# Agent attention with a top-1 mixture of experts: the second layer's high and low products into the same columns

## The chip, the cores and the metric

One NeuronCore of a Trainium2 chip runs the whole kernel. The metric is device microseconds for one execution, as the median of several runs. PE (TensorE) multiplies matrices into PSUM, which has eight banks of 512 float32 per partition; ACT (ScalarE), DVE (VectorE) and POOL (GpSimd) work on 128 partitions beside it, POOL on SBUF alone here; SP (SyncE) issues most DMAs. A matmul on PE has its stationary operand ("weights") loaded first by a separate instruction, which the profile lists as an engine of its own, PEld.

## The reference

Four batches of 11,456 tokens with 128 channels go through attention to 49 agents, and the result through a mixture of eight experts of which each token uses one.

```python
a2k = softmax(scale * agents @ k.T)          # 49 agents over the keys
agent_v = a2k @ v
x = softmax(scale * q @ agents.T) @ agent_v  # 45824 tokens x 128
logits = x @ w_gate
e = argmax(logits)                           # one expert for a token
gate_w = softmax(logits)[e]
eom = sigmoid(x @ w_output_gate)[e]
h = relu(x @ w1[e])                          # 1024 hidden
out = gate_w * eom * (h @ w2[e])             # 128
```

All of it is float32.

## The kernel before, in words

For each batch the kernel finds the expert that most tokens of the batch use (the dominant one) and runs every token through it. Tokens of other experts are gathered, run through their own expert in float32 and scattered over the result later: the left-over path (`left_...`, tiles `let`, `lx`, `lh`, `ly`, `lw`, `bigs`). Its index tables are made from gathers with indirect DMAs on POOL and comparisons on DVE.

A batch has twelve units of up to 1,024 tokens. For each unit there are small float32 products with 50 columns: `ks` (agents by keys), `av` (weights by values), `qs` (queries by agents). DVE, ACT and POOL make softmax weights of them; a DMA turns those (`x_ld<-e`), and a half-precision product with 36 columns, `lg`, gives gates and logits. From these comes `smt`, one factor for each token, which holds the softmax's denominator, the gates and the scaling of the half-precision operands.

The main work is two layers on 92 tiles of up to 512 tokens (four groups of 128, a few of 96 or fewer groups), all in half precision with each float32 operand as a high and a low part.

- First layer, `mm1`: half a tile's hidden units at a time, four blocks of 128, in the four PSUM banks 0 to 3: four matmuls `h<-x_ld,w` with 128 rows, then four with 19 rows. Then `relu` makes of each block `hh` (ACT, the high part) and `hl` (DVE, the low part: relu less hh). A ring of 16 blocks (`RING`), two tiles, holds them.
- Second layer, `mm2(i, k, f)`: hidden block f of tile i, in two passes k over the eight blocks, each for 256 tokens (two groups j). A pass has a PSUM bank `y`; group j has 256 columns of it. For each j one matmul takes hh as weights and 256 columns of `vv` (w2's high part, then its low part), and one takes hl as weights and the 128 columns of the high part, into the first 128 columns. These two matmuls are called a step below; there are 2,880 steps.
- `finish(i, k)`: ACT copies the low columns (`ys`), DVE adds them to the high columns (`os`), and the bank is free. After the second pass `store` waits for `smt`, POOL multiplies the tile by it, and SP stores it.

The order on every engine is set when the program is built, by a planner (`Clock`, `Engine`). It keeps a virtual time for each engine, with a cost for each instruction, and issues an instruction when its inputs are ready by that time. Main stream: `main_stream` issues a second-layer block while the first layer is more than `OFF` = 8 blocks ahead, otherwise half a tile of the first layer if there is room in the ring and the four banks are free by the plan. After each matmul `tick` lets one float32 product through ("heavy") or some light work; it stands between the two matmuls of a step. So small products are spread between second-layer matmuls. All work goes through one helper, so the profile's line is L193 for nearly everything, and groups are told apart by tile names.

Of the kernel before, what the change touches and what calls it, by code (L numbers as in the profile page):

```python
# [7 lines left out]
F32 = mybir.dt.float32  # L8
# [3 lines left out]
AF = mybir.ActivationFunctionType  # L12
ALU = mybir.AluOpType
# [3 lines left out]
P = 128  # L17
B, N, C, A, E, F = 4, 11456, 128, 49, 8, 1024
A2 = 50
NB = F // P  # L20
# [2 lines left out]
NTOK = B * N  # L23
SCALE = 1.0 / float(C) ** 0.5

YS = 2

LARGE, SMALL, KEEP = 8, 8, 4
PHASES = [(0, 3, 13, 384), (3, 1, 1, 128)]
# [5 lines left out]
G4 = 4  # L35
# [207 lines left out]
def agent_attention_top1_moe(ctx, tc, qT, kT, v, aT, wg, wo, w1, w2, cst, out):  # L243
    nc = tc.nc
    clk = Clock()
    ACT, DVE, POOL = Engine(clk, "ACT", nc.scalar), Engine(clk, "DVE", nc.vector), Engine(clk, "POOL", nc.gpsimd)
    PE, SY = Engine(clk, "PE", nc.tensor), Engine(clk, "SP", nc.sync)

    def pool(name, bufs):
        return Tiles(clk, ctx.enter_context(tc.tile_pool(name=name, bufs=bufs)), bufs)  # L250
# [3 lines left out]
    wk = pool("wk", 2)  # L254
# [34 lines left out]
    def release(k):  # L289
        banks[k][0] = True  # L290
# [130 lines left out]
    SM = {}  # L421
# [5 lines left out]
    def spawn(g, prio=2):  # L427
        streams.append([prio, len(streams), g, None])
        streams.sort(key=lambda x: x[0])

    def tick(heavy=1, light=2):

        clk.slots = [heavy, 0]
        for x in list(streams):
            if x[3] is not None and x[3][0] == "PE" and clk.can(x[3], x[0]):
                step(x)
        clk.slots = [0, light]
        for x in list(streams):
# [558 lines left out]
    tiles = []  # L997
# [4 lines left out]
    NT = len(tiles)  # L1002
    OFF = 8
    RING = 16
    H = {}
    Y = {}
    done, summed = set(), set()

    def mm1(i, hf):

        b, u, h, pp, n = tiles[i]
        w = pp * n
        own_, rest = state[b]["w"][hf]
        x1, x2 = (x[:, 512 * h:512 * h + w] for x in X1[b, u])
        p = []
        for g in range(G4):
            p.append((bank(f"h{i}_{hf}_{g}", k=g), hold()))
            PE.matmul(p[g][0][:, 0:w], own_[:, g * P:(g + 1) * P], x1, start=True, stop=False)
            if g < G4 - 1:
# [18 lines left out]
        release(mark)  # L1038
        H[i, f] = hh, hl

    def mm2(i, k, f):

        b, u, h, pp, n = tiles[i]
        hh, hl = H[i, f] if 2 * k + 2 < n else H.pop((i, f))
        vv = state[b]["vv"][f // 4]
        if f == 0:
            Y[i, k] = bank(f"y{i}_{k}"), hold()
        for j in range(2):
            y = Y[i, k][0][0:pp, j * 2 * C:(j + 1) * 2 * C]
            sl = slice((2 * k + j) * pp, (2 * k + j + 1) * pp)  # L1050
            PE.matmul(y, hh[:, sl], vv[:, f % 4].rearrange("p h c -> p (h c)"), start=(f == 0 and j == 0),
                      stop=False)
            tick()
            PE.matmul(y[:, 0:C], hl[:, sl], vv[:, f % 4, 0, :], start=False, stop=(f == NB - 1 and j == 1))
            tick(0, 1)
        if f == NB - 1:
            spawn(finish(i, k), 0)

    OS = {}

    def finish(i, k):
        b, u, h, pp, n = tiles[i]
        if k == 0:
            while i > 3 and i - 4 not in done or i > 1 and i - 2 not in summed:
                yield None
            OS[i] = wk.tile([P, 4, C], F32, name=f"os{i}", tag="os", bufs=4)
        os = OS[i]
        y, mark = Y.pop((i, k))
        yv = y.rearrange("p (j h c) -> p j h c", h=2, c=C)
        ol = wk.tile([P, 2, C], F32, name=f"ys{i}_{k}", tag="ys", bufs=YS)  # L1070
        yield from ACT.q.copy(ol[0:pp], yv[0:pp, :, 1, :])
        yield from DVE.q.tensor_tensor(os[0:pp, 2 * k:2 * k + 2, :], yv[0:pp, :, 0, :], ol[0:pp], op=ALU.add)
        release(mark)
        if 2 * k + 2 == n:
            summed.add(i)
            spawn(store(i, os))

    def store(i, os):
        b, u, h, pp, n = tiles[i]
        while (b, u) not in SM:  # L1080
            yield None
        smt = SM[b, u]
        yield from POOL.q.tensor_tensor(os[0:pp, 0:n, :], os[0:pp, 0:n, :],
                                        smt[0:pp, 4 * h:4 * h + n].unsqueeze(2).broadcast_to([pp, n, C]),
                                        op=ALU.mult)
        base, _, nt = UNITS[u]
        r0 = b * N + base
        dst = out[r0:r0 + pp * nt, :].rearrange("(p t) c -> p t c", t=nt)[:, 4 * h:4 * h + n, :]
        yield from SY.q.dma_start(dst, os[0:pp, 0:n, :])
        done.add(i)  # L1090

    def main_stream():
        first_ = [(i, hf) for i in range(NT) for hf in range(2)]
        second_ = [(i, k, f) for i in range(NT) for k in range(tiles[i][4] // 2) for f in range(NB)]
        m1 = m2 = freed = 0
        while m2 < len(second_):
            can1 = can2 = False
            now = clk.now()
            if m1 < len(first_) and G4 * (m1 + 1) - freed <= RING and group_free() is not None and group_free() <= now + 20.0:
                i, hf = first_[m1]  # L1100
                b, u, h, pp, n = tiles[i]
                can1 = (b, u) in X1 and rests[NU * b + u] > 1 and b in state and len(state[b]["w"]) > hf
                can1 = can1 and clk.at([*X1[b, u], *state[b]["w"][hf]]) <= now + 20.0
            i, k, f = second_[m2]
            if (i, f) in H:
                vv = state[tiles[i][0]]["vv"]
                can2 = len(vv) > f // 4 and clk.at([H[i, f][1], vv[f // 4]]) <= now
                can2 = can2 and (f > 0 or n_free() > 1)
            if can2 and (G4 * m1 > NB * i + (NB * k + f) / (tiles[i][4] // 2) + OFF or not can1):
                mm2(i, k, f)  # L1110
                m2 += 1
                if (i, f) not in H:
                    freed += 1
# [408 lines left out]
```

## Time and profile before

| | |
|---|---|
| median of 3 runs | 1071.93 us (1071.73 to 1074.43) |
| the profiled execution's own time | 1073.62 us |
| its span, first to last instruction | 1071.6 us |
| busy: PE, DVE, ACT, POOL | 1033.2, 859.9, 592.6, 275.2 us |
| mean granted TensorE clock | 0.984 |
| instructions | 27,654 |

A page of the profile describes one execution. A group row gives line, engine, operation, output and inputs with sizes, the count, then busy time and the mean of one in ns, then the idle time ahead of such instructions and who ended it. A row of the waits gives who waited for whom, the total, how often, and the longest. A row of the timeline gives start, duration, engine and operation. Records of matmuls overlap, since they are pipelined: the distance from start to start says what a matmul costs. Some matmul records are missing from a trace.

The granted clock is 1.0 for most of the span. PE has work from the first stage, in which keys are loaded and the first agents are made, to the end, since `AHEAD`, `MIX` and the planner spread the batches' small products over the second layer's steps.

### The profile page before, as it was taken

How to read it: one execution, taken by the hardware profiler on the slowest of the kernel's cores; microseconds unless marked ns; L12 is line 12 of the kernel's file. 1: busy time of each engine (PE TensorE's matmuls, PEld its weight loads, DVE VectorE, ACT ScalarE, POOL GpSimd, SP SyncE). 2: the span in 40 equal slices, each digit the busy share in tenths (PEclk: the TensorE clock that was granted, in tenths of full speed). 3: DMA queues.
4: the chain of work that ended last, by engine and by line, in shares of the span. 5: the costliest groups of instructions: out<-in, count | busy, mean ns of one | idle time of the engine just before them, and what ended most of it. 6: DMA issues, size and time to landing. Idle time of an engine off the chain costs nothing. (4 is left out here: it accounts for less than half of the span.)

```text
span 1071.6 us, 27654 instructions
## 1 busy us (share of the span) xinstructions
PE 1033.2 (96%) x10671; PEld 840.9 (78%) x10671; DVE 859.9 (80%) x2344; ACT 592.6 (55%) x1396; POOL 275.2 (26%) x440
## 2 busy tenths in 40 slices
PE   9989899999999999999999999999899999999996
PEld 9977777788788877778788788777677676788885
DVE  2738699888988898888988888989989978877551
ACT  2325456565755665556755665556645554655552
POOL 0301123222121232232121232321123263521121
PEclk9999899999999999999999999999999998999998
DMA  8785854444557444453466544446232732644430
GB/s 293 231 213 156 193 117 146 125 122 136 133 141 197 141 134 112 119 147 116 111 185 166 153 125 119 129 123 171 73 75 56 168 92 78 149 136 130 131 124 28
DMA packets 108818, 147.13 MB, mean 137 GB/s; under 512 B 61128, under 2 KB 71548, under 8 KB 108682
## 3 DMA queue, kind: packets, MB, share of 16 engines
q1 hardware_dynamic: 107338, 143.83, 48.4%
q0 software_dynamic: 1344, 1.49, 0.8%
q8 instruction: 85, 1.39, 0.5%
q14 instruction: 51, 0.42, 0.1%
HBM read 91.86 MB, written 35.17 MB: 119 GB/s over the span
## 5 line engine op out<-in xcount | busy, mean ns | idle before, releaser
L193 PE MATMUL y<-vv,hh 128*128 128x256 f16 (+1 forms) x2880 | 593.0, 275 | 4.3 <-DVE w L193 3.1
L193 PE MATMUL y<-vv,hl 128*128 128x128 f16 (+1 forms) x2880 | 532.7, 220 | 3.3 <-DVE hl L193 2.5
L193 DVE SCALAR_TENSOR_TENSOR hl<-h,hh 128x512 f16<-128x512 f32 (+1 forms) x736 | 447.0, 667 | 85.3 <-ACT hh L193 84.2
L193 ACT ACTIVATE hh<-h 128x512 f16<-128x512 f32 (+1 forms) x736 | 372.2, 591 | 231.3 <-PE h L193 231.0
L193 PEld LDWEIGHTS <-hh 128*128 128x128 f16 (+1 forms) x2880 | 284.7, 99 | 67.0 <-issue 37.1
L193 PEld LDWEIGHTS <-hl 128*128 128x128 f16 (+1 forms) x2880 | 320.7, 112 | 10.9 <-DVE hl L193 6.2
L193 PE MATMUL h<-x_ld,w 128*128 128x512 f16 (+1 forms) x1472 | 289.4, 379 | 12.1 <-DVE hl L193 11.5
L193 PEld LDWEIGHTS <-w 128*128 128x128 f16 x1472 | 98.3, 103 | 105.0 <-issue 84.7
L193 POOL TENSOR_TENSOR os<-os,smt 128x512 f32<-128x512 f32 (+1 forms) x92 | 94.3, 1025 | 234.8 <-issue 168.9
L193 ACT COPY ys<-y 128x256 f32<-128x256 f32 x180 | 67.4, 374 | 99.6 <-PE y L193 97.4
L193 PEld LDWEIGHTS qs<-at,q_ld 128*128 128x128 f32 x720 | 112.0, 190 | 7.0 <-DVE km_m L193 0.3
L193 PE MATMUL qs<-at,q_ld 128*128 128x50 f32 x720 | 114.0, 245 | 0.0
L193 PE MATMUL ks<-at,k_ld 128*128 128x50 f32 x720 | 111.4, 257 | 2.2 <-DMA k_ld<-kT 2.2
L193 PEld LDWEIGHTS ks<-at,k_ld 128*128 128x128 f32 x720 | 109.2, 195 | 5.5 <-DMA k_ld<-kT 3.1
L193 PE MATMUL av<-ev,v_ld 128*128 128x50 f32 x720 | 110.7, 251 | 0.0
L193 PEld LDWEIGHTS av<-ev,v_ld 128*128 128x128 f32 x720 | 107.6, 191 | 1.8 <-ACT ev L193 0.2
L193 DVE TENSOR_TENSOR os<-y,ys 128x256 f32<-128x256 f32 x180 | 75.0, 417 | 30.3 <-ACT ys L193 22.4
L193 POOL TENSOR_TENSOR e<-ef,e 128x392 f16<-128x392 f32 (+1 forms) x48 | 41.8, 870 | 151.9 <-ACT e L193 93.4
L193 POOL TENSOR_TENSOR ev<-S,km_o 128x400 f32<-128x400 f32 (+1 forms) x44 | 41.1, 935 | 150.7 <-PE av L193 108.6
L193 POOL TENSOR_SCALAR smt<-lT,i 128x8 f32<-128x8 f32 (+1 forms) x48 | 14.8, 309 | 130.6 <-DVE lT L193 109.9
L193 PEld LDWEIGHTS <-idle_x 128*128 128x128 f16 x305 | 45.9, 158 | 2.7 <-DVE idle_x L193 1.1
L193 PE MATMUL lh<-lxs,lw 128*128 128x128 f32 x224 | 42.9, 276 | 0.0
(200 smaller groups left out, 1041.3 us busy)
## 6 DMA issues: line engine op xcount, KB each, us to landing
q_ld<-qT SPq DMA_DIRECT2D x44, 512.0 KB
v_ld<-v SPq DMA_DIRECT2D x44, 512.0 KB
out<-os SPq DMA_DIRECT2D x88, 256.0 KB
k_ld<-kT SPq DMA_DIRECT2D x43, 512.0 KB
lw<-w SPq DMA_DIRECT2D x28, 512.0 KB
efd<-ef SPq DMA_DIRECT2D x44, 200.0 KB
x_ld<-x_ld SPq DMA_DIRECT2D x176, 38.0 KB
w1t<-w SPq DMA_DIRECT2D x8, 256.0 KB
```

The costliest lines, as they stand in the source:

```text
L193: return getattr(self.eng, op)(*a, **k)
```

## The change

The second layer has one pass over a tile instead of two, and a tile has one bank `y`: its four groups j have 128 columns each. For each j and hidden block three matmuls, all with 128 columns, add into the same columns: hh by w2's high part, hh by w2's low part (hh is loaded again, as each matmul loads its own weights), hl by w2's high part. `tick` is where it was: the heavy one ahead of the hl matmul, the light one behind it.

At the end of a tile ACT reads the bank in four pieces and multiplies each by its column of `smt` on the way, straight into the tile that is stored. The copy on ACT, the addition on DVE and the multiplication on POOL go. The wait for `smt` moves from `store`, behind the bank's release, to `finish`, ahead of it.

A block hh, hl is given back as soon as its one use is over; before, it was held until the second pass. A new tile's first block starts with one free bank left where it asked for two.

```diff
-    def mm2(i, k, f):
+    def mm2(i, f):
...
-        hh, hl = H[i, f] if 2 * k + 2 < n else H.pop((i, f))
+        hh, hl = H.pop((i, f))
...
-        for j in range(2):
-            y = Y[i, k][0][0:pp, j * 2 * C:(j + 1) * 2 * C]
-            sl = slice((2 * k + j) * pp, (2 * k + j + 1) * pp)
-            PE.matmul(y, hh[:, sl], vv[:, f % 4].rearrange("p h c -> p (h c)"), start=(f == 0 and j == 0),
-                      stop=False)
+        for j in range(n):
+            y = Y[i][0][0:pp, j * C:(j + 1) * C]
+            sl = slice(j * pp, (j + 1) * pp)
+            PE.matmul(y, hh[:, sl], vv[:, f % 4, 0, :], start=(f == 0 and j == 0), stop=False)
+            PE.matmul(y, hh[:, sl], vv[:, f % 4, 1, :], start=False, stop=False)
             tick()
-            PE.matmul(y[:, 0:C], hl[:, sl], vv[:, f % 4, 0, :], start=False, stop=(f == NB - 1 and j == 1))
+            PE.matmul(y, hl[:, sl], vv[:, f % 4, 0, :], start=False, stop=(f == NB - 1 and j == n - 1))
             tick(0, 1)
...
-        ol = wk.tile([P, 2, C], F32, name=f"ys{i}_{k}", tag="ys", bufs=YS)
-        yield from ACT.q.copy(ol[0:pp], yv[0:pp, :, 1, :])
-        yield from DVE.q.tensor_tensor(os[0:pp, 2 * k:2 * k + 2, :], yv[0:pp, :, 0, :], ol[0:pp], op=ALU.add)
-        release(mark)
...
+        while i > 3 and i - 4 not in done or (b, u) not in SM:
+            yield None
+        os = wk.tile([P, 4, C], F32, name=f"os{i}", tag="os", bufs=4)
+        y, mark = Y.pop(i)
+        smt = SM[b, u]
+        for j in range(n):
+            yield from ACT.q.activation(os[0:pp, j, :], y[0:pp, j * C:(j + 1) * C], AF.Copy,
+                                        scale=smt[0:pp, 4 * h + j:4 * h + j + 1])
+        release(mark)
+        spawn(store(i, os))
...
-        while (b, u) not in SM:
-            yield None
-        smt = SM[b, u]
-        yield from POOL.q.tensor_tensor(os[0:pp, 0:n, :], os[0:pp, 0:n, :],
-                                        smt[0:pp, 4 * h:4 * h + n].unsqueeze(2).broadcast_to([pp, n, C]),
-                                        op=ALU.mult)
...
-            if m1 < len(first_) and G4 * (m1 + 1) - freed <= RING and group_free() is not None and group_free() <= now + 20.0:
+            if m1 < len(first_) and G4 * (m1 + 1) - m2 <= RING and group_free() is not None and group_free() <= now + 20.0:
...
-                can2 = can2 and (f > 0 or n_free() > 1)
-            if can2 and (G4 * m1 > NB * i + (NB * k + f) / (tiles[i][4] // 2) + OFF or not can1):
+                can2 = can2 and (f > 0 or n_free() > 0)
+            if can2 and (G4 * m1 > m2 + OFF or not can1):
```

In the order of the instructions that the prediction shows, `h42_0_3` is block 3 of the first half of tile 42's hidden layer, `y41` a bank of the second layer, `hh41_7` the high part of hidden block 7 of tile 41; the last number of a name only tells buffers apart.

More of the change, by code (lines that the diff above doesn't have):

```diff
@@ L24 @@
 SCALE = 1.0 / float(C) ** 0.5
-YS = 2
 LARGE, SMALL, KEEP = 8, 8, 4
@@ L1006, in agent_attention_top1_moe @@
     Y = {}
-    done, summed = set(), set()
+    done = set()
     def mm1(i, hf):
@@ L1039, in relu @@
         H[i, f] = hh, hl
-    def mm2(i, k, f):
+    def mm2(i, f):
         b, u, h, pp, n = tiles[i]
-        hh, hl = H[i, f] if 2 * k + 2 < n else H.pop((i, f))
+        hh, hl = H.pop((i, f))
         vv = state[b]["vv"][f // 4]
         if f == 0:
-            Y[i, k] = bank(f"y{i}_{k}"), hold()
-        for j in range(2):
-            y = Y[i, k][0][0:pp, j * 2 * C:(j + 1) * 2 * C]
-            sl = slice((2 * k + j) * pp, (2 * k + j + 1) * pp)
-            PE.matmul(y, hh[:, sl], vv[:, f % 4].rearrange("p h c -> p (h c)"), start=(f == 0 and j == 0),
-                      stop=False)
+            Y[i] = bank(f"y{i}"), hold()
+        for j in range(n):
[3 more added lines that the diff above has]
+            PE.matmul(y, hh[:, sl], vv[:, f % 4, 1, :], start=False, stop=False)
@@ L1053, in mm2, with finish @@
             tick()
-            PE.matmul(y[:, 0:C], hl[:, sl], vv[:, f % 4, 0, :], start=False, stop=(f == NB - 1 and j == 1))
+            PE.matmul(y, hl[:, sl], vv[:, f % 4, 0, :], start=False, stop=(f == NB - 1 and j == n - 1))
             tick(0, 1)
         if f == NB - 1:
-            spawn(finish(i, k), 0)
-    OS = {}
-    def finish(i, k):
+            spawn(finish(i), 0)
+    def finish(i):
         b, u, h, pp, n = tiles[i]
-        if k == 0:
-            while i > 3 and i - 4 not in done or i > 1 and i - 2 not in summed:
-                yield None
[L1066 to L1069, printed above, removed]
-        ol = wk.tile([P, 2, C], F32, name=f"ys{i}_{k}", tag="ys", bufs=YS)
-        yield from ACT.q.copy(ol[0:pp], yv[0:pp, :, 1, :])
-        yield from DVE.q.tensor_tensor(os[0:pp, 2 * k:2 * k + 2, :], yv[0:pp, :, 0, :], ol[0:pp], op=ALU.add)
+        while i > 3 and i - 4 not in done or (b, u) not in SM:
[6 more added lines that the diff above has]
+                                        scale=smt[0:pp, 4 * h + j:4 * h + j + 1])
@@ L1073, in finish @@
         release(mark)
-        if 2 * k + 2 == n:
-            summed.add(i)
-            spawn(store(i, os))
+        spawn(store(i, os))
     def store(i, os):
         b, u, h, pp, n = tiles[i]
-        while (b, u) not in SM:
-            yield None
-        smt = SM[b, u]
-        yield from POOL.q.tensor_tensor(os[0:pp, 0:n, :], os[0:pp, 0:n, :],
-                                        smt[0:pp, 4 * h:4 * h + n].unsqueeze(2).broadcast_to([pp, n, C]),
-                                        op=ALU.mult)
@@ L1093, in main_stream @@
         first_ = [(i, hf) for i in range(NT) for hf in range(2)]
-        second_ = [(i, k, f) for i in range(NT) for k in range(tiles[i][4] // 2) for f in range(NB)]
-        m1 = m2 = freed = 0
+        second_ = [(i, f) for i in range(NT) for f in range(NB)]
+        m1 = m2 = 0
         while m2 < len(second_):
@@ L1103, in main_stream @@
                 can1 = can1 and clk.at([*X1[b, u], *state[b]["w"][hf]]) <= now + 20.0
-            i, k, f = second_[m2]
+            i, f = second_[m2]
             if (i, f) in H:
@@ L1107, in main_stream @@
                 can2 = len(vv) > f // 4 and clk.at([H[i, f][1], vv[f // 4]]) <= now
-                can2 = can2 and (f > 0 or n_free() > 1)
-            if can2 and (G4 * m1 > NB * i + (NB * k + f) / (tiles[i][4] // 2) + OFF or not can1):
-                mm2(i, k, f)
+                can2 = can2 and (f > 0 or n_free() > 0)
+            if can2 and (G4 * m1 > m2 + OFF or not can1):
+                mm2(i, f)
                 m2 += 1
-                if (i, f) not in H:
-                    freed += 1
             elif can1:
```

## The prediction

> **What bounds the kernel now.** I read the page first, then the busy time by stage, the waits of PE, and the timeline where PE runs unbroken.
>
> ```profile
> PE 1033.2 (96%) x10671; PEld 840.9 (78%) x10671; DVE 859.9 (80%) x2344; ACT 592.6 (55%) x1396; POOL 275.2 (26%) x440
> ```
>
> ```profile
> 160.00:725.00 565.00, 558.24 (x5974) 452.09 (x5973) 495.29 (x1321) 339.70 (x793) 144.26 (x240) 1.00 0.49 137
> ```
>
> The page's busy line, then the middle stage (its length, the busy time of PE, PEld, DVE, ACT and POOL, the granted clock). From 160 to 725 us PE is busy for 558.2 of 565 us at full clock. DVE is second with 495.3, ACT has 339.7. So a matmul that takes longer moves the end by as much, and a cheaper DVE, ACT or POOL pays only where PE now waits for it. The waits of PE (total, times, longest):
>
> ```profile
> PE h L193 <- DVE hl L193: 11.5, 33, 3.6
> PE lg L193 <- DMA x_ld<-e: 3.7, 1, 3.7
> ...
> PE y L193 <- DVE hl L193: 2.5, 3, 1.5
> ...
> PE y L193 <- DVE os L193: 1.1, 2, 0.6
> ```
>
> The first is the first layer: its matmuls find their four banks still unread by DVE. All that DVE causes here and the change could touch (hl for h, hl for y, os) is 11.5 + 2.5 + 1.1 = 15.1 us. That is the most there is to win on this side.
>
> **The matmuls.** Second layer in the timeline, 500.50 to 500.73, then one pair at the end of the unbroken stage:
>
> ```profile
> 500.50 0.22 PE L193 MATMUL y<-vv,hl 128*128 128x128 f16 x1
> 500.50 0.10 PEld L193 LDWEIGHTS <-hh 128*128 128x128 f16 x1
> 500.56 0.27 PE L193 MATMUL y<-vv,hh 128*128 128x256 f16 x1
> 500.56 0.10 PEld L193 LDWEIGHTS <-hl 128*128 128x128 f16 x1
> 500.67 0.22 PE L193 MATMUL y<-vv,hl 128*128 128x128 f16 x1
> ...
> 724.78 0.22 PE L193 MATMUL y<-vv,hl 128*128 128x128 f16 x1
> 724.84 0.27 PE L193 MATMUL y<-vv,hh 128*128 128x256 f16 x1
> ```
>
> Columns are start, duration, engine. A duration (0.22, 0.27) holds the pipeline; what counts is start to start. Between 160 and 725 us, 1,589 hl matmuls are followed directly by an hh one (the first at 161.22, the last the pair above): 55.9 ns on average for 128 columns. The 256 columns take 109 ns (500.56 to 500.67). A step now costs 165 ns. The change makes three 128-column matmuls of it: 3 x 55.9 = 167.7, 2.7 ns more. The page has the steps:
>
> ```profile
> L193 PE MATMUL y<-vv,hh 128*128 128x256 f16 (+1 forms) x2880 | 593.0, 275 | 4.3 <-DVE w L193 3.1
> L193 PE MATMUL y<-vv,hl 128*128 128x128 f16 (+1 forms) x2880 | 532.7, 220 | 3.3 <-DVE hl L193 2.5
> L193 PEld LDWEIGHTS <-hh 128*128 128x128 f16 (+1 forms) x2880 | 284.7, 99 | 67.0 <-issue 37.1
> ```
>
> 2,880 x 2.7 = **+7.7 us**, all on PE. (The waits of this stage left the granted clock at 1.00, so short waits cost themselves and no more.)
>
> The same weights hh are loaded a second time, in 2,880 loads more. The order of PE shows it, behind the first half of tile 42's hidden layer, before and then now.
>
> ```order
> L193 MATMUL h42_0_3_9316<-x21_9_ld_7920,w1_0_4872 128x512
> L193 LDWEIGHTS hh41_0_9135
> L193 MATMUL y41_0_9335<-vv1_0_4860,hh41_0_9135 128x256
> L193 MATMUL avn2_9322<-kc_71,avd_0_87 49x128
> L193 LDWEIGHTS hl41_0_9136
> L193 MATMUL y41_0_9335<-vv1_0_4860,hl41_0_9136 128x128
> ```
>
> ```order
> L192 MATMUL h42_0_3_10581<-x21_9_ld_8873,w1_0_5466 128x512
> L192 LDWEIGHTS hh41_7_10493
> L192 MATMUL y41_10391<-vv1_1_5451,hh41_7_10493 128x128
> L192 LDWEIGHTS hh41_7_10493
> L192 MATMUL y41_10391<-vv1_1_5451,hh41_7_10493 128x128
> L192 LDWEIGHTS hl41_7_10494
> L192 MATMUL y41_10391<-vv1_1_5451,hl41_7_10494 128x128
> ```
>
> Two things moved: hh stands twice, and behind this group PE is already at the last block (7) of tile 41, where it was at the first (0). The load costs nothing if it hides behind a 128-column matmul. The hh load of 500.50 does just that (it starts with the hl matmul, and the next matmul starts 0.06 later), and behind 36 columns a load costs even less:
>
> ```profile
> 451.81 0.10 PEld L193 LDWEIGHTS <-x_ld 128*128 128x128 f16 x1
> 451.87 0.18 PE L193 MATMUL lg<-gs,x_ld 128*128 128x36 f16 x1
> 451.87 0.10 PEld L193 LDWEIGHTS <-hh 128*128 128x128 f16 x1
> 451.89 0.27 PE L193 MATMUL y<-vv,hh 128*128 128x256 f16 x1
> ```
>
> From lg to y with a load of its own: 0.02 us. The small float32 products often stand behind the 256-column matmul, and will stand behind a 128-column one. That is seen too, and it starts after 0.06:
>
> ```profile
> 453.91 0.22 PE L193 MATMUL y<-vv,hl 128*128 128x128 f16 x1
> 453.97 0.38 PE L193 MATMUL av<-ev,v_ld 128*128 128x50 f32 x2
> ```
>
> So I add nothing for loads. The Trainium skill speaks against the change here: "TensorE: Matmul & The Clock Gate", section "Back-to-back issue gap", gives about 81 ns for each 128-column matmul in a stream of load and matmul pairs. By that a step would cost 243 ns, 78 more than now, or 225 us in all, as an estimate from that page. The 55.9 ns, measured with a load per matmul, disagree, and I go by them.
>
> **The end of a tile.** Removed: 180 copies on ACT, 180 additions on DVE, 92 products on POOL. Added: 360 scaled copies on ACT, of a form that the left-over path already has.
>
> ```profile
> L193 ACT COPY ys<-y 128x256 f32<-128x256 f32 x180 | 67.4, 374 | 99.6 <-PE y L193 97.4
> L193 DVE TENSOR_TENSOR os<-y,ys 128x256 f32<-128x256 f32 x180 | 75.0, 417 | 30.3 <-ACT ys L193 22.4
> L193 POOL TENSOR_TENSOR os<-os,smt 128x512 f32<-128x512 f32 (+1 forms) x92 | 94.3, 1025 | 234.8 <-issue 168.9
> L193 ACT ACTIVATE bigs<-ly,bigs 128x128 f32<-128x128 f32 x14 | 5.2, 373 | 2.8 <-PE ly L193 2.5 <-issue 0.4
> ```
>
> DVE loses 75.0 us and POOL 94.3. ACT gains 360 x 0.373 - 67.4 = 67 us in records, less where they follow each other; at 592.6 us it has the room. But the four stand in one row on ACT. At the end of tile 42, with the next tile's relus behind, before (of its first pass) and now:
>
> ```order
> L193 ACTIVATE eo2_0_9581<-ogs2_0_9555 128x8
> L193 COPY lL2_1_9567<-lg2_1_9517 128x128
> L193 COPY ys42_0_9602<-y42_0_9488 128x256
> L193 ACTIVATE hh43_4_9637<-h43_1_0_9610 128x512
> L193 ACTIVATE hh43_5_9640<-h43_1_1_9618 128x512
> ```
>
> ```order
> L192 COPY lL2_1_10816<-lg2_1_10777 128x128
> L192 ACTIVATE os42_10833<-y42_10620,smt1_9_9210 128x128 x4
> L192 ACTIVATE hh43_4_10898<-h43_1_0_10877 128x512
> L192 ACTIVATE hh43_5_10901<-h43_1_1_10884 128x512
> L192 ACTIVATE hh43_6_10903<-h43_1_2_10889 128x512
> ```
>
> One copy of 0.37 stood ahead of the relus, and now four. Four relus take 2.06 (next part) at some 0.6 each, so they start 0.49 apart and overlap by 0.11; a scaled copy then takes 0.37 - 0.11 = 0.26 of ACT's time, and three more of them 0.78. The scaled copies also wait for smt, for which only POOL waited; it is ready a tile earlier, so I cost that at nothing (if it were late, the relus behind, and then PE, would wait).
>
> The lighter DVE should be on time for the h banks. Of the 11.5 us I leave the 3.6 (DVE itself waits there for a gather), so **-7.9**; the two waits for os go, **-1.1**. PE meets the late x_ld (3.7) later: 75 steps of y stand ahead of that lg before, 88 now, 13 x 0.165 = **-2.1**.
>
> **What is late next.** A block of hh and hl is freed as soon as it is used, not in a tile's second pass. So the second layer runs closer behind the first. By the order, 21 of 184 half-tiles now have 12 or fewer y matmuls between their last h matmul and the first y that needs them; 2 had 8 or fewer, the same work, before. Tile 42's block 7 ends and its own block 0 follows:
>
> ```order
> L192 LDWEIGHTS hl41_7_10494
> L192 MATMUL y41_10391<-vv1_1_5451,hl41_7_10494 128x128
> L192 LDWEIGHTS hh42_0_10587
> L192 MATMUL y42_10620<-vv0_0_5449,hh42_0_10587 128x128
> L192 LDWEIGHTS hh42_0_10587
> ```
>
> Those 12 matmuls are 0.67 us of PE. What the new block needs meanwhile is in the trace where DVE was free (first the page's rows for one relu and one hl, which form hh and hl):
>
> ```profile
> L193 DVE SCALAR_TENSOR_TENSOR hl<-h,hh 128x512 f16<-128x512 f32 (+1 forms) x736 | 447.0, 667 | 85.3 <-ACT hh L193 84.2
> L193 ACT ACTIVATE hh<-h 128x512 f16<-128x512 f32 (+1 forms) x736 | 372.2, 591 | 231.3 <-PE h L193 231.0
> ```
>
> ```profile
> 598.50 1.38 PE L193 MATMUL h<-x_ld,w 128*128 128x512 f16 x8
> 599.91 2.06 ACT L193 ACTIVATE hh<-h 128x512 f16<-128x512 f32 x4 [1.17 <-PE h L193]
> 600.54 1.89 DVE L193 SCALAR_TENSOR_TENSOR hl<-h,hh 128x512 f16<-128x512 f32 x3 [0.73 <-ACT hh L193]
> ```
>
> From the end of h (598.50 + 1.38 = 599.88) to the end of the first hl are 1.34 us: an hl takes 0.67 (short forms included), so the first ends at 601.21 or a little later. PE would wait 1.34 - 0.67 = 0.67 us. In 13 of the 21 nothing else stands between: 13 x 0.67 = **+8.7 us**; in the other 8 small products fill the time. Bounds: none if h is done early enough at all of them; 21 x 0.67 = 14.1, and as much again if DVE runs late there. It does run late at times:
>
> ```profile
> 438.92 0.98 DVE L193 TENSOR_TENSOR ld<-ll,lm 128x64 f32<-128x64 f32 x1
> 439.83 0.93 DVE L193 TENSOR_TENSOR sm<-sm,s 128x50 f32<-128x50 f32 x1
> ...
> L193 DVE TENSOR_TENSOR ld<-ll,lm 128x64 f32<-128x64 f32 x44 | 14.6, 332 | 0.3
> ```
>
> 0.98 against a mean of 0.33: POOL was in its own products then. Of those the change takes away only the os ones. The Trainium skill ("SBUF — State Buffer", "Who interferes with whom") says that a DVE instruction with two SBUF inputs and a GpSimd one that reads SBUF exclude each other; the rows fit.
>
> **The end.** The last y starts at 1059.13, with seven small products (1.78 us) behind it; POOL's last os ends at 1060.95, when PE ends too.
>
> ```profile
> 1059.13 0.22 PE L193 MATMUL y<-vv,hl 128*96 128x128 f16 x1
> 1059.19 1.78 PE L193 MATMUL ly<-lw,lh 128*128 128x128 f32 x14
> 1060.35 0.60 POOL L193 TENSOR_TENSOR os<-os,smt 96x256 f32<-96x256 f32 x1 [3.66 <-DVE more L193]
> ```
>
> Now the small products are done two tiles earlier and y is last; two scaled copies follow it, 0.26 and 0.37, which end 0.6 to 0.7 after PE: **+0.7 us**.
>
> **The sum.** The profiled execution took 1073.6 us (span 1071.6 and 2.0 around it), 1.7 above the median of 1071.9. 1073.6 + 7.7 - 7.9 - 1.1 - 2.1 + 8.7 + 0.7 = 1079.6; less 1.7 that is 1077.9, so 1078 as a median. A measurement here tells 0.3%, 3.2 us: same is 1068.7 to 1075.1.
>
> **Rivals.**
> - *No new wait for hl*: without the 8.7 the sum gives 1069. For it: 160 to 725 us has little PE idle, and the planner that sets the order knows the relus' length. Against: the 0.67 us. Chance 0.2, within 0.3%.
> - *Faster: DVE and POOL freed*: no DVE wait is left at all. 15.1 go instead of 9.0, none come: 1073.6 + 7.7 + 0.7 - 15.1 - 2.1 - 1.7 = 1063. It decides if DVE, 75 us lighter, is never behind at h or y. Against: part of the lag comes from products of POOL that stay, and the 3.6 hangs on a gather. Chance 0.17.
> - *ACT and DVE late together*: the four scaled copies ahead of the relus (0.78 more than one copy's slot) and a blocked DVE meet the short distances: 21 x 0.67 x 2 = 28 instead of 8.7 at worst; half of the 19 added gives 1088. Slower. Chance 0.16.
> - *Loads don't overlap*: three records of 0.1 us one after another make 0.30 a step, 0.135 more, +390 us. The overlapping records at 500.50 and 500.56 speak against it; 0.02.
>
> The forecast itself has 0.45, nearly all above 1075.1. Faster 0.17; same 0.2 and a little of the forecast, 0.22; slower 0.61. The range reaches from next to the faster case, 1064, to a little over the late one, 1091.
>
> **What would show it.** Right: y steps of 0.168; y waits for hl of some 10 us in many short pieces, h waits for hl under 5; DVE near 785 busy, POOL near 181, ACT near 660. Wrong: hh to hh over 0.06 (loads), or y waits for hl still near 2.5 (no short distance felt), or a chain that ends with ACT and smt.

## The result, and the profile after

The changed kernel takes 1114.82 us (median, 1112.73 to 1115.90), the kernel before, run beside it, 1073.18 us (1071.73 to 1074.60). The ratio is 1.0386, with a 95% interval of 1.0361 to 1.0411: 41.6 us slower. The side was forecast, the size was not; 1114.82 lies above the range.

Most of the forecast lines came as they were worked out. First the page of the kernel after (busy times, and the groups that the change touches), then the busy time from 160 to 725 us in the columns of the prediction:

```profile
PE 1073.5 (97%) x13551; PEld 916.6 (83%) x13551; DVE 787.2 (71%) x2164; ACT 627.8 (57%) x1576; POOL 179.0 (16%) x348
...
L192 PE MATMUL y<-vv,hh 128*128 128x128 f16 (+1 forms) x5760 | 600.7, 220 | 2.0 <-issue 1.6
...
L192 PE MATMUL y<-vv,hl 128*128 128x128 f16 (+1 forms) x2880 | 537.3, 220 | 15.2 <-DVE hl L192 13.1
...
L192 PE MATMUL qs<-at,q_ld 128*128 128x50 f32 x720 | 129.5, 266 | 0.8 <-issue 0.8
...
L192 ACT ACTIVATE os<-y,smt 128x128 f32<-128x128 f32 x360 | 104.2, 387 | 29.1 <-PE y L192 27.6
```

```profile
160.00:725.00 565.00, 562.81 (x7461) 479.83 (x7458) 440.83 (x1159) 347.89 (x873) 82.78 (x174) 1.00 0.47 132
```

DVE and POOL are as light as forecast (787 and 179 us), and in the middle stage PE is busy for 562.8 of 565 us, more than before. Over the whole span PE is idle for 37.5 us, 38.4 before. So the 41.6 us are not idle time of PE; PE itself has more to do. The waits of PE in the kernel after say the same:

```profile
PE y L192 <- DVE hl L192: 13.1, 16, 4.4
PE y L192 <- issue: 3.7, 7, 1.1
PE lg L192 <- DMA x_ld<-e: 2.6, 1, 2.6
```

The wait of h for hl (11.5 us before) is gone, y now waits for hl for 13.1 us instead of 2.5. By these rows the exchange is about even, as it was forecast. From start to start it isn't. Here h waits in the kernel before:

```profile
655.72 0.76 PE L193 MATMUL h<-x_ld,w 128*128 128x512 f16 x2
656.70 0.38 PE L193 MATMUL h<-x_ld,w 128*128 128x512 f16 x1 [0.22 <-DVE hl L193]
657.30 0.38 PE L193 MATMUL h<-x_ld,w 128*128 128x512 f16 x1 [0.22 <-DVE hl L193]
```

The second of the first two starts at 656.10 (0.38 before their end), so the last three are 0.60 apart, where two h matmuls that wait for nothing are 0.216 apart (the median). Each of the waits costs 0.38 us, of which the row counts 0.22: the record of the matmul ahead (0.38) covers 0.16 of it and counts it as busy. Summed over the starts, the late h matmuls cost 19.0 us in the trace of before and nothing in that of after (at full granted clock); late hl matmuls of y cost 6.2 and 18.1. So the waits gave back some 7 us, and PE's own work must have grown by more than the 41.6.

The one group that grew without having been touched is that of the small float32 products. A qs pass takes 266 ns on average (245 before; av, ks, lh and ly grew as well). Here they are in the timeline, first the kernel before, a product behind the 256-column matmul, and the product's weight loads (PEld):

```profile
451.49 0.27 PE L193 MATMUL y<-vv,hh 128*128 128x256 f16 x1
451.60 0.32 PE L193 MATMUL qs<-at,q_ld 128*128 128x50 f32 x2
451.76 0.21 PE L193 MATMUL lg<-gs,x_ld 128*128 128x36 f16 x2
```

```profile
451.49 0.30 PEld L193 LDWEIGHTS qs<-at,q_ld 128*128 128x128 f32 x2
```

Then the kernel after, the same place in a step, and the weight loads beneath it:

```profile
304.34 0.28 PE L192 MATMUL y<-vv,hh 128*128 128x128 f16 x2
304.45 0.38 PE L192 MATMUL qs<-at,q_ld 128*128 128x50 f32 x2
304.66 0.22 PE L192 MATMUL y<-vv,hl 128*128 128x128 f16 x1
```

```profile
304.28 0.15 PEld L192 LDWEIGHTS <-hh 128*128 128x128 f16 x2
304.39 0.30 PEld L192 LDWEIGHTS qs<-at,q_ld 128*128 128x128 f32 x2
304.55 0.17 PEld L192 LDWEIGHTS <-hl 128*128 128x128 f16 x1
```

A product is two matmul passes (x2), each with a weight load of its own. Before, 0.16 us pass from its start (451.60) to the next matmul (451.76); after, 0.21 (304.45 to 304.66), and the row of its two passes is 0.06 longer (0.38 for 0.32). The loads tell why: the first of them begins at 304.39, when the second hh matmul begins (0.056 behind the first), not earlier, though the first hh matmul runs from 304.34. In the kernel before it begins at 451.49, with the 256-column matmul right ahead. Counted from the start of the matmul right ahead of the product, it is the same in both kernels: 451.49 to 451.76 is 0.27, and 304.39 to 304.66 is 0.27 too. Over all such places in the two traces the median is 0.268 us in both (844 and 868 places). This holds for the products with 50 columns, most of them; for those with 128 (lh, ly) the distance is 0.333, again in both kernels. Two loads of 0.112 (the pace of passes in a row, shown with e4_quads below) are 0.224 of it; what is left, 0.044 and 0.109, goes with the product's own columns. So a product occupies the weight path for two loads, and only the one matmul right ahead of it lies beside them. That matmul took 0.109 us of the 0.268 before and takes 0.056 now; the other half of the old 256 columns is now an extra matmul that lies beside nothing.

By the order of PE 861 products stood behind a 256-column matmul before and 20 behind one of 128 columns; now 885 stand behind one of 128 columns. 865 x 0.056 = 48 us, of which 2.3 (2.7 ns each) are in the prediction's 7.7 already: some 46 are new.

### The profile page after: what moved, and what is told of

Same layout as the page of the kernel before. It is cut to its first block, busy times and chain, and to the rows that moved or that the text cites. A ratio compares the mean times of both kernels' runs of the same rounds, so it can differ in the third digit from the quotient of the medians.

```text
span 1111.0 us, 33313 instructions
## 1 busy us (share of the span) xinstructions
PE 1073.5 (97%) x13551; PEld 916.6 (83%) x13551; DVE 787.2 (71%) x2164; ACT 627.8 (57%) x1576; POOL 179.0 (16%) x348
## 5 line engine op out<-in xcount | busy, mean ns | idle before, releaser
L192 PE MATMUL y<-vv,hh 128*128 128x128 f16 (+1 forms) x5760 | 600.7, 220 | 2.0 <-issue 1.6
L192 PE MATMUL y<-vv,hl 128*128 128x128 f16 (+1 forms) x2880 | 537.3, 220 | 15.2 <-DVE hl L192 13.1
L192 PEld LDWEIGHTS <-hh 128*128 128x128 f16 (+1 forms) x5760 | 436.6, 99 | 43.0 <-issue 38.9
L192 PE MATMUL qs<-at,q_ld 128*128 128x50 f32 x720 | 129.5, 266 | 0.8 <-issue 0.8
L192 PE MATMUL av<-ev,v_ld 128*128 128x50 f32 x720 | 122.2, 266 | 0.0
L192 PE MATMUL ks<-at,k_ld 128*128 128x50 f32 x720 | 121.2, 267 | 0.2 <-DMA k_ld<-kT 0.2
L192 ACT ACTIVATE os<-y,smt 128x128 f32<-128x128 f32 x360 | 104.2, 387 | 29.1 <-PE y L192 27.6
L192 POOL TENSOR_TENSOR e<-ef,e 128x392 f16<-128x392 f32 (+1 forms) x48 | 41.6, 867 | 304.9 <-issue 243.6
L192 ACT ACTIVATE ef<-qz 128x392 f32<-128x392 f32 (+1 forms) x48 | 25.0, 520 | 51.3 <-DVE qz L192 34.9
L192 PE MATMUL lh<-lxs,lw 128*128 128x128 f32 x224 | 48.1, 296 | 0.0
L192 PE MATMUL ly<-lw,lh 128*128 128x128 f32 x224 | 47.7, 295 | 0.0
```

The source lines that it names most:

```text
L192: return getattr(self.eng, op)(*a, **k)
```

## The experiments

The theory, called A in the first expectations and D, in its corrected form, in the later ones, is the lost cover. Of the rivals in the first ones, B blames what comes with the one pass over the blocks of the hidden layer (y close behind h, the scaled copies on ACT), which the first two kernels don't have, and C the second load of hh, which e2_split has and e1_slot hasn't. "Before" below is always the kernel before, run beside it on the same chip.

**Only the place of the products moved (e1_slot).** The kernel before, with a product behind the 128-column hl matmul instead of the 256-column hh one:

```diff
             PE.matmul(y, hh[:, sl], vv[:, f % 4].rearrange("p h c -> p (h c)"), start=(f == 0 and j == 0),
                       stop=False)
-            tick()
+            tick(0, 1)
             PE.matmul(y[:, 0:C], hl[:, sl], vv[:, f % 4, 0, :], start=False, stop=(f == NB - 1 and j == 1))
-            tick(0, 1)
+            tick()
```

> The kernel before, with nothing changed but the place in the step where a float32 product is let in: behind the 128-column hl matmul, not behind the 256-column hh matmul. Theory A (cover): a float32 product loads its weights twice, each load holds the load path for 0.11 us, and a 55.9 ns matmul ahead covers only half of the first, so its second half starts 0.10 us after its first where it was 0.044: 0.056 us more each. By the order 874 products stand behind 128 columns, 20 did before: 854 x 0.056 = 47.8 us, less up to 12 us of waits for DVE that a slower PE no longer has: 1109 to 1121 us. Theory B (short distance: the loss is in waits for hl and in the row of scaled copies on ACT) and theory C (the second load of hh is what costs): nothing of theirs is in this kernel, 1069 to 1077 us.

Measured: 1114.73 us, before 1071.47, ratio 1.0393 (1.0348 to 1.0437): 43.3 us for a change that adds no instruction and takes none away. In its timeline:

```profile
450.38 0.27 PE L193 MATMUL y<-vv,hh 128*128 128x256 f16 x1
450.49 0.22 PE L193 MATMUL y<-vv,hl 128*128 128x128 f16 x1
450.55 0.38 PE L193 MATMUL av<-ev,v_ld 128*128 128x50 f32 x2
450.76 0.27 PE L193 MATMUL y<-vv,hh 128*128 128x256 f16 x1
```

The same 0.38 and 0.21 as in the changed kernel, and 0.27 from 450.49 to 450.76. The time lies in theory A's range. Moving the products alone makes a loss of that size; B and C fall as the main cause.

**The matmul split, two passes kept (e2_split).** The kernel before, with the 256 columns as two matmuls of 128 into columns of their own, hh loaded twice:

```diff
-            PE.matmul(y, hh[:, sl], vv[:, f % 4].rearrange("p h c -> p (h c)"), start=(f == 0 and j == 0),
-                      stop=False)
+            PE.matmul(y[:, 0:C], hh[:, sl], vv[:, f % 4, 0, :], start=(f == 0 and j == 0), stop=False)
+            PE.matmul(y[:, C:2 * C], hh[:, sl], vv[:, f % 4, 1, :], start=False, stop=False)
```

> The kernel before, with the 256-column matmul cut into two of 128 columns that load hh twice and write the same 256 columns; two passes, DVE's addition and POOL's product stay. Theory A: 2,880 x 2.7 ns = 7.7 us, and 865 float32 products behind 128 columns against 20: 845 x 0.056 = 47.3, less up to 12 us of waits that go: 1116 to 1128 us. If it comes out at or below the changed kernel's 1115, the lighter DVE and POOL were worth nothing there. Theory B: no short distances here (2 half-tiles of 184), so 1081 us. Theory C: 1115 or more.

Measured: 1121.69, ratio 1.0453 (1.0402 to 1.0505). That is in theory A's range, and 7.0 us over e1_slot, which has lost the same covers: the price of three matmuls for two, the second load of hh included. The forecast had 7.7. The 7.0 is less sure than it looks, since the granted clock of these runs is 0.983 in the median and that of e1_slot's 0.990, which can be worth up to 8 us by itself (0.007 of 1122, an estimate); the 0.056 from hh to hh in the trace is the firmer sign. It stands 50.2 us over before, the changed kernel 41.6.

**Products in pairs and in fours (e4_pairs, e4_quads).** The changed kernel, with the same number of places for products, but two in a row behind every second hh, or four behind the last hh of a block. The edit for the pairs:

```diff
-            tick()
+            if j % 2:
+                tick()
+                tick()
+            else:
+                tick(0, 2)
```

> The changed kernel, with two float32 products let in at every second step instead of one at every step; the second stands behind the first, whose second half lasts 0.11 us and covers a load. Theory A: 494 products behind 128 columns against 885: 391 x 0.056 = 21.9 us less, 1093 us, 1088 to 1098. Theory B: 1115, as the waits for hl stay, or 2 to 4 less where the order has fewer short distances. Theory C: 1115, as every reload is still there.

> The changed kernel, with four float32 products let in at the end of a hidden block (every fourth step) instead of one at every step. Theory A: 280 products behind 128 columns against 885: 605 x 0.056 = 33.9 us less, 1081 us, 1075 to 1087; clusters may bring waits of their own. Theory B: half-tiles with a short distance are 10 instead of 21, so at most 8 us less, 1107 to 1115. Theory C: 1115.

Measured: 1103.06 (ratio 1.0291, 1.0247 to 1.0335) and 1108.40 (1.0336, 1.0289 to 1.0383). They stand 31.6 and 36.9 us over before, the changed kernel 41.6: a gain, but less than half and about a seventh of what was expected, and the row of four shows that it is no gain of cover:

```profile
306.54 0.28 PE L192 MATMUL y<-vv,hh 128*128 128x128 f16 x2
306.65 1.04 PE L192 MATMUL qs<-at,q_ld 128*128 128x50 f32 x8
307.53 0.22 PE L192 MATMUL y<-vv,hl 128*128 128x128 f16 x1
```

Eight passes from 306.65 to 307.53 are 0.88 us, 0.11 each: a pass is no cover for the loads of the next product. That part of theory A fell, and it became D: two loads of 0.112 us for each product, of which the one matmul right ahead covers as much as it lasts itself. What the pairs gained fits their waits (y for hl 5.0 us instead of 13.1).

**A size between (e5_192).** The kernel before with 192 columns in the hh matmul of blocks 1 to 7, which leaves out half of the low part there:

```diff
-            PE.matmul(y, hh[:, sl], vv[:, f % 4].rearrange("p h c -> p (h c)"), start=(f == 0 and j == 0),
-                      stop=False)
+            cw = 2 * C if f == 0 else 3 * C // 2
+            PE.matmul(y[:, 0:cw], hh[:, sl], vv[:, f % 4].rearrange("p h c -> p (h c)")[:, 0:cw],
+                      start=(f == 0 and j == 0), stop=False)
```

> The kernel before with one size changed: in blocks 1 to 7 the hh matmul has 192 columns instead of 256, so half of the low part of those blocks is left out. Theory D (a float32 product needs the weight path for 2 x 0.112 us, and only the matmul right ahead hides part of it, as much as it lasts itself): 192 columns last 0.082, so a product behind them takes 0.268 - 0.082 = 0.186 us from its start to the next matmul, where it takes 0.158 behind 256. Of 2,520 shortened matmuls 636 have a product behind them by the order and save nothing; the others save 0.027 each, 51 us, so 1021 us and, with PE faster, up to 20 us more waits for DVE. Rival E (what counts is some number of columns from which the second load is hidden, and 192 are enough): 0.158 behind 192, and 68 us saved, 1004 and the same waits. The start-to-start time decides, the whole time only if it lies at an end.

The timeline decides for D: 300.82 to 301.08 is 0.26 (0.268 in the median again), and from the product's start to the next matmul 0.18, between the 0.16 behind 256 columns and the 0.21 behind 128.

```profile
300.82 0.25 PE L193 MATMUL y<-vv,hh 128*128 128x192 f16 x1
300.90 0.35 PE L193 MATMUL ks<-at,k_ld 128*128 128x50 f32 x2
301.08 0.22 PE L193 MATMUL y<-vv,hl 128*128 128x128 f16 x1
```

The whole time missed both forecasts: 1070.96, before 1074.53, ratio 0.9967 (0.9945 to 0.9988). Of the 51 us that PE should have saved, 4 came out. Its busy times and waits:

```profile
PE 997.9 (94%) x10671; PEld 816.8 (77%) x10671; DVE 873.3 (82%) x2344; ACT 588.1 (55%) x1396; POOL 274.1 (26%) x440
```

```profile
PE h L193 <- DVE hl L193: 15.5, 64, 1.2
PE lg L193 <- DMA x_ld<-e: 11.6, 6, 5.1
PE y L193 <- DVE hl L193: 8.5, 6, 3.6
PE y L193 <- DVE os L193: 5.0, 3, 2.1
```

PE is 35 us less busy, and these four waits are 40.6 us where they were 18.8. The granted clock was lower too, 0.975 in the median of these runs against 0.985 beside them, which can be worth up to 11 us (0.010 of 1071, an estimate). So PE bounds the kernel before only just: the rest stands right behind.

**The end of a tile alone (e3_pool, e8_act).** Two passes, 256 columns and all covers stay. In e3_pool ACT scales the low columns, DVE scales the high ones and adds, POOL's product is gone; in e8_act ACT scales both and POOL adds. The main part of the edit of e8_act:

```diff
-        yield from ACT.q.copy(ol[0:pp], yv[0:pp, :, 1, :])
-        yield from DVE.q.tensor_tensor(os[0:pp, 2 * k:2 * k + 2, :], yv[0:pp, :, 0, :], ol[0:pp], op=ALU.add)
+        c0 = 4 * h + 2 * k
+        for j in range(2):
+            for o, x in (os[0:pp, 2 * k + j, :], yv[0:pp, j, 0, :]), (ol[0:pp, j, :], yv[0:pp, j, 1, :]):
+                yield from ACT.q.activation(o, x, AF.Copy, scale=SM[b, u][0:pp, c0 + j:c0 + j + 1])
         release(mark)
+        yield from POOL.q.tensor_tensor(os[0:pp, 2 * k:2 * k + 2, :], os[0:pp, 2 * k:2 * k + 2, :], ol[0:pp], op=ALU.add)
```

> The kernel before with the end of a tile changed alone: ACT copies the low columns already scaled by smt, DVE multiplies the high ones by smt and adds in one instruction, POOL's product is gone. Two passes, 256 columns and all places of products stay. Theory D: the covers are the same, so the time can only fall by waits, of which DVE and POOL cause 15 us at most: 1060 to 1072. Rival (the relief of POOL and DVE was worth more than the waits show): under 1058. Rival (the longer DVE instructions and the wait for smt in ACT's row cost): over 1075.

> The kernel before with only the end of a tile changed: ACT copies high and low columns scaled by smt (four copies of 128 columns a pass), POOL adds the two, DVE's addition and POOL's product are gone. Two passes, 256 columns and the places of the products stay, so this is the second half of the change (ScalarE scales out of the bank, DVE lighter) without the first. DVE falls from 860 by 75 us or more, ACT rises from 593 to some 730. Theory D with F (the covers are kept, and DVE, which stands right behind PE, gives up its 11.5 us of waits for h and 1 for os): 1056 to 1068. Rival (four copies in ACT's row delay the relus, and PE waits for ACT and hl): over 1076.

Measured: e3_pool 1078.76, before 1074.53, ratio 1.0036 (1.0015 to 1.0057), a little slower: outside the range of D, on the side of the rival that its longer DVE instructions or the wait for smt cost something. e8_act 1062.37, before 1071.17, ratio 0.9926 (0.9900 to 0.9952), 8.8 us faster, within its range, and faster than both kernels of this case. The busy times of e3_pool, then of e8_act with its waits:

```profile
PE 1035.2 (96%) x10671; PEld 845.5 (79%) x10671; DVE 868.5 (81%) x2524; ACT 633.8 (59%) x1576; POOL 180.1 (17%) x348
```

```profile
PE 1023.3 (97%) x10671; PEld 839.9 (79%) x10671; DVE 807.0 (76%) x2164; ACT 725.5 (69%) x1936; POOL 310.7 (29%) x528
```

```profile
PE y L193 <- DVE hl L193: 6.1, 5, 4.0
PE lg L193 <- DMA x_ld<-e: 2.9, 1, 2.9
...
PE h L193 <- DVE hl L193: 2.4, 8, 0.6
```

e3_pool takes 95 us from POOL and gives DVE 9 more, and it is slower; e8_act takes 53 us from DVE and gives POOL 36 and ACT 133 more, and it is faster. So DVE's relief is what the end of a tile seems to be worth; POOL's shows no gain, though e3_pool mixes it with the 9 us more on DVE and doesn't show it alone. In e8_act the waits of h for hl fall from 11.5 to 2.4, by the starts from 19.0 to 4.3, while y's for hl grow from 6.2 to 10.1. The same matmuls keep PE busy for 9.9 us less (1023.3 for 1033.2), since the covered part of a wait counts as busy; in part it is the granted clock of this execution (0.989 for 0.984).

**Fewer products behind 128 columns (e6_half, e11_mix).** The changed kernel with a product behind every second y step (e6_half: `tick(j % 2)`), or behind every fourth and also behind the last matmul of a group of h (e11_mix):

```diff
             PE.matmul(p[g][0][:, 0:w], rest[rows, g * P:(g + 1) * P], x2[rows, :], start=False, stop=True)
+            tick(g // 3)
...
-            tick()
+            tick(j // 3)
```

> The changed kernel with a product allowed behind every second y step only (odd sub-tiles), one at a time as before. By the order 783 products stand behind 128 columns instead of 885, the others move behind the 512-column matmuls. Theory D: 102 x 0.055 = 5.6 us less, and with longer distances between h and y (25 of 184 half-tiles under 3 us of work instead of 44) some 5 of the 13 us of waits for hl: 1099 to 1107. If the waits don't follow the distance: 1107 to 1111. Rival (what counts is only how many products there are, not where): 1112 to 1117.

> The changed kernel with products behind only every fourth y step, and one more place behind the last of the eight 512-column matmuls of a group. By the order 541 products stand behind 128 columns instead of 885. Theory D: 344 x 0.055 = 19 us less, 1096, and the waits of y for hl decide the rest: 1085 if they go as in e6_half, 1105 if the shorter distances (71 half-tiles under 2 us of work, 25 in the changed kernel) cost 0.2 us each. Rival (places don't matter): 1112 to 1117.

Measured: e6_half 1098.63, ratio 1.0213 (1.0173 to 1.0253), just under the lowest of what was expected (1099); some 102 products moved behind the long h matmuls, and y waits 9.4 us for hl. It stands 24.1 us over before, 17.5 less than the changed kernel. Of these 6 are the cover and 4 that wait; the other 7 I can't assign. e11_mix 1121.42, ratio 1.0455 (1.0429 to 1.0481): slower than any of its forecasts. Its timeline shows what the forecast had missed:

```profile
311.51 0.71 PE L192 MATMUL h<-x_ld,w 128*128 128x512 f16 x5
312.15 0.30 PEld L192 LDWEIGHTS qs<-at,q_ld 128*128 128x128 f32 x2 [0.23 <-issue]
312.15 0.42 PE L192 MATMUL qs<-at,q_ld 128*128 128x50 f32 x2
312.41 0.28 PE L192 MATMUL y<-vv,hh 128*128 128x128 f16 x2
```

The last four of these five h matmuls have 19 rows, and a product behind them takes 0.26 us to the next matmul (312.15 to 312.41), more than behind 128 columns. The product's first load begins with the product itself. So these 512 columns cover nothing. And y waits for hl more often:

```profile
PE y L192 <- DVE hl L192: 14.7, 27, 2.8
```

Where products stand matters, but moving them also moves the distance between the layers.

**One pass with the covers kept (e7_two, e9_twoact).** A tile in two banks, one pass, 256-column matmuls with products behind them; the end of a tile as in e3_pool and as in e8_act. The part of the edit on the banks:

```diff
-            Y[i] = bank(f"y{i}"), hold()
-        for j in range(n):
-            y = Y[i][0][0:pp, j * C:(j + 1) * C]
+            Y[i] = []
+            for k in range(n // 2):
+                Y[i].append((bank(f"y{i}_{k}"), hold()))
+        for j in range(n):
+            y = Y[i][j // 2][0][0:pp, j % 2 * 2 * C:(j % 2 + 1) * 2 * C]
```

> One pass as in the changed kernel, but the high and low parts in columns of their own again, a tile's 512 tokens in two banks, with 256-column matmuls ahead of the products, and the end of a tile as in e3_pool. hh isn't loaded twice. Theory D: 839 products stand behind 256 columns by the order (861 before), so the loss of 40 us is gone with one pass kept: 1058 to 1076, as e3_pool within 8 us. Rival (the one pass itself costs, as y runs closer behind h): over 1085.

> The kernel of e7_two (one pass, two banks for a tile) with the end of a tile of e8_act. Why was e7_two 52 us slower with its products covered? Theory G: two y banks beside four of h leave too few, and the next y waits until DVE has added (os: 9.0 us of waits in all, and small products that find no bank); ACT frees the banks earlier here: 1070 to 1100. Rival (the one pass itself costs): 1115 to 1135.

Measured: e7_two 1126.54, ratio 1.0494 (1.0463 to 1.0525); e9_twoact 1156.20, ratio 1.0794 (1.0765 to 1.0823). Both miss the forecasts of D and G; e7_two lies on the side of its rival, that the one pass itself costs, and e9_twoact above both of its ranges. The first waits of e7_two, then that of e9_twoact:

```profile
PE lg L192 <- DMA x_ld<-e: 9.7, 2, 6.3
PE y L192 <- DVE os L192: 9.0, 7, 2.7
```

```profile
PE y L192 <- ACT ys L192: 28.1, 28, 2.2
```

The next y does wait for a bank in both, but freeing the banks by ACT made it worse, not better, so G as it was put fell. The covers are there in e7_two (a product still takes 0.268 us from the start of the 256 columns), and PE is idle for 70 us of its span, 38 before, at a mean granted clock of 0.973 instead of 0.984. Whether the second bank or the single pass is to blame stays open. The changed kernel holds one bank for a tile, and in its trace no wait of y for a bank stands out.

**DVE lighter under the 192 columns (e10_192act).** e5_192 with the end of e8_act:

> The kernel of e5_192 (192 columns in blocks 1 to 7, half of the low part of those blocks left out) with the end of a tile of e8_act. Why did e5_192 gain 4 us and not 51? Theory F: DVE was busy for 92% of the middle stage there, and what PE saved went into waits for it; with 75 us less on DVE the gain comes out: 1022 to 1045. Rival (the loads x_ld or the small products' own chain hold the pace): 1055 to 1072.

Measured: 1056.18, ratio 0.9852 (0.9816 to 0.9889). 15.0 us under before, little more than e8_act and e5_192 give each by itself (8.8 + 3.6 = 12.4), and in the range of the rival. So F (what PE saved went into waits for DVE alone) fell too: the longest wait is now that for ACT, in the banks that it copies from.

```profile
PE y L193 <- ACT ys L193: 19.6, 19, 2.0
PE lg L193 <- DMA x_ld<-e: 5.5, 4, 2.0
```

## Why the prediction was wrong, point by point

The runs add up in size. Lost covers 43.3 (e1_slot), the split 7.0 (e2_split less e1_slot), the lighter end of a tile -8.8 (e8_act): together 41.5, measured 41.6. That they agree to 0.1 is luck: each is a difference of medians some 3 to 5 us wide, on different chips and at slightly different granted clocks, and the end of a tile in e8_act isn't quite that of the changed kernel. Nor does it show that the one pass is free. In the changed kernel more of the waits of h went than in e8_act, and more waits of y for hl came, and these two nearly cancel; e7_two, one pass with its covers kept, is 52 us slower than before, which stays unexplained.

- *Three matmuls of 55.9 ns for 165, +7.7.* Right: 7.0, and hh to hh is 0.056 in the trace. The Trainium skill's 81 ns for a pair of load and matmul ("TensorE: Matmul & The Clock Gate", "Back-to-back issue gap") doesn't hold for this kernel's f16 pairs; the prediction was right to go by the trace.
- *The second load of hh at nothing.* Right; the hh pairs run on at 0.056.
- *DVE on time for h, -7.9, and os, -1.1.* Right in kind: e8_act, with a lighter DVE and the covers kept, gained 8.8. Too small in size: in the changed kernel the wait of h went altogether, in part because PE is slower (it was 7.5 in e1_slot, where DVE's work is the same), and it was worth 19.0 us from start to start, not the 11.5 of the row. So "15.1 us, the most there is to win on this side" was too low as well.
- *y closer behind h, +8.7.* Right in kind and nearly in size: the wait grew from 2.5 to 13.1, by 10.6, with one of 4.4 in it; from start to start it grew by 11.9.
- *x_ld later, -2.1.* It was 1.1 (3.7 to 2.6).
- *The end, +0.7.* The scaled copies end 0.7 us behind PE, as forecast, but from the end of PE's last matmul to the end of the span it is 12.7 us instead of 10.6, so +2.1.
- *ACT, DVE and POOL.* 627.8, 787.2 and 179.0 for some 660, 785 and 181. The scaled copies keep ACT busy for 104.2 us, less than their 0.37 each adds up to, as they overlap more than was reckoned.
- *The small float32 products behind 128 columns: "it starts after 0.06", so "I add nothing for loads".* **This is the step that failed.** The start of the product was looked at, not its end. The row on which it rested has 0.38 for two passes, where a product behind 256 columns has 0.32, and 0.06 times 865 products, some 50 us, was there to be read. What the runs showed in place of nothing: a product covers only as much of its two loads as the one matmul right ahead lasts, so it takes 0.21 us to the next matmul where it took 0.16. That is 43.3 us in e1_slot and some 46 in the sum of the changed kernel.
- *The rivals.* None had this. "The loads don't overlap" was priced for 2,880 loads of hh at 390 us; they do overlap. What doesn't is the second load of a product, where the change had not touched an instruction.

With 46 us for the products, and the waits of h and y as measured from start to start (19.0 for 7.9, 11.9 for 8.7), x_ld and the end as above (1.1 for 2.1, 2.1 for 0.7), the sum of 1079.6 becomes 1120 us for the profiled execution, which took 1112.73. Of the 7 us that are left I can't say where they lie.

The check in the prediction, hh to hh over 0.06, would not have found it either: that distance came out as forecast.

## What to carry to other kernels

A long matmul is a cover for the weight loads of what stands behind it: before it is cut in two, look up what follows each one in PE's order, and compare the start of the *next* matmul after that, behind a long and behind a short one, in the trace of before. Both cases often stand there already, as the 20 products behind 128 columns did here, and the rarer row, times the count it will have, is the price. A row of the waits has the same trap: it counts from the end of a record, and pipelined records hide a part of each wait (0.16 of 0.38 us here), so price a wait by the starts too. And where an engine bounds a kernel by a few per cent only, what it saves is mostly given to the next in line: here some 50 us off PE's work were worth 4, and 53 us off DVE's were worth 9.

## What the runs showed of the hardware

- A float32 product with 128 rows and columns of weights and 50 moving columns takes two passes with two loads of 0.112 us, and from the start of the matmul right ahead to the matmul behind it passes 0.268 us, whether the one ahead is of 128, 192 or 256 columns; eight passes in a row take 0.11 each. By the Trainium skill's formula, columns / 1.2 ns, a load of 128 columns takes 107 ns as an estimate ("TensorE: Matmul & The Clock Gate", "LDWEIGHTS (loading the stationary operand)"), with which these float32 loads agree. The Trainium skill also excludes FP32 from the fast load (the same page, "Weight-path perf modes — Fast Weight Load (FWL) and DoubleRow").
- An f16 load of the same 128 columns, on the other hand, doesn't show between f16 matmuls: 0.056 us from one 128-column matmul with a load to the next.
- Sums of three matmuls into the same 128 columns of a bank, one right behind the other, run at the same 0.056 us.
- Behind the four h matmuls of 19 rows a product took 0.26 us to the next matmul, though each has 512 columns, and its first load began with the product (312.15 in e11_mix).
- A matmul held up by a wait started 0.60 us behind the one ahead instead of 0.216, and the wait's row counts 0.22 of these 0.38 us.
